# The first two groups of a gated linear attention kernel, worked in chunks of 128 steps in place of groups of 256

## The chip, the cores and the metric

One NeuronCore of one Trainium2 chip. The metric is the device time of one execution in microseconds, as the median of several runs. A profiled execution gives the trace; its span, from the first to the last instruction, is a little shorter than its device time.

## What is computed

Inputs: `q`, `k`, `v`, `alpha` of shape (4, 8, 768, 48) (batch, heads, steps, head dimension), all float32, and the weights `w_in` (384 x 1024), `A_log` (512) and `w_out` (512 x 384), which arrive as float64.

```python
for t in range(S):                        # attention, per batch and head
    state = alpha[t][:, None] * state + outer(k[t], v[t])
    y[t] = q[t] @ state
x = y laid out as (B, S, H*D)             # 384 wide
val, gate = split(x @ w_in)               # 512 each
for t in range(S):
    h = exp(A_log)[0] * h + val[t];  ys[t] = h      # the reference uses one decay
out = (gate * sigmoid(gate) * ys) @ w_out
```

## The kernel before

The function `fast` does the work; `general` is a second program for inputs that its checks turn away, and isn't touched. The 4 x 768 steps are 12 groups `m` of 256 steps, three groups to a batch, and a group is two chunks `c` of 128. Heads lie in pairs: four pairs `p` of two heads, 64 columns each of which 48 are used, so a chunk of one quantity is a tile of 128 rows (two heads) by 4 x 128 columns (pair, step).

The recurrence is taken apart through running products of alpha. For each group, `products(m)` (line 616) runs on DVE: a small multiply puts the start value into `first` (626), a memset sets alpha's first column of each pair to zero (627), a scan of 1024 columns makes `prod` (629), then `ratio` (636 or 638) and a reciprocal (640) are taken from its end, and a scan backwards of 1025 columns makes `inv` (641). Keys are multiplied by `inv` and queries by `prod` into `Z` (603). Then, chunk by chunk:

- `scores` (668): eight products on PE of keys and queries into two PSUM banks, `sc[0]` and `sc[1]`.
- `masks` (678): DVE multiplies bank 0 by the causal mask (687, called the near mask below); ACT copies bank 1 to SBUF (685) and POOL multiplies it there by the mask (686, the far mask). For chunk (0, 1) DVE does both (683).
- `keys` (659): PE turns the keys back, ACT copies them out (666).
- `values` (689): PE adds masked scores times v into `y`; its second half uses what POOL masked.
- `state` (713): PE adds to the running state `st`, ACT copies it out (722); `carried` (701) adds the part of `y` that comes from the earlier state.
- `join` (724): ACT copies `y` out, and eight small DMAs lay it out as `xT`.

`project`, `hidden`, `gate` and `output` (747 to 800) are the second half, on which PE works for most of the time. The weights' 64-bit words are turned into float32 by `low_word` on ACT, `high_word` on DVE and `word_sum` on POOL (508 to 535).

The first three groups, and no others, are loaded in their natural order and turned by PE: `natural_alpha` (572) and `natural_qk` (589). Alpha of a group is copied from PSUM into `aT` (584 on ACT, 586 on DVE); keys and queries are multiplied straight out of PSUM.

The whole is under a manual schedule: every engine runs its instructions in the order in which the program emits them, and waits where a tile isn't ready. For the start this order is written out in lines 814 to 902: the loads on SP (and two on ACT), the constants (476), then alpha of group 0, its products, keys and queries, group 1's first products, group 0's scores, masks, values and state, `join(0)`, the rest of group 1, `join(1)`. Between them stand six `warm` matmuls of 512 columns (827), whose results aren't used. [...]

Of the kernel before, what the change touches and what calls it, by code (L numbers as in the profile page):

```python
# [341 lines left out]
FIRST_PRODUCT = 1e18  # L342
# [4 lines left out]
def fast(  # L347
# [118 lines left out]
    alphas = aT[:, 0:4 * GC].rearrange("p (h n) -> p h n", h=4)  # L466
    prods = prod.rearrange("p (h n) -> p h n", h=4)
    invs = inv[:, 1:].rearrange("p (h n) -> p h n", h=4)
    ratio = const.tile([C, N, 4], FP32, name="ratio")
    above = const.tile([C, N], FP32, name="above")  # L470
    wmin = const.tile([C, NW], FP32, name="wmin")
# [2 lines left out]
    flag = const.tile([1, 1], I32, name="flag")  # L474

    def constants():
        for m, engine in ((0, nc.vector), (1, nc.gpsimd)):
            if m:
                make_identity(nc, ident)

                nc.gpsimd.memset(mask, 1.0)
                nc.gpsimd.affine_select(out=mask, in_=mask, compare_op=ALU.is_ge, fill=0.0, base=0,
                                        channel_multiplier=-1, pattern=[[1, C]])
                for t in vs:
                    nc.gpsimd.memset(t[:, :, :, D:64], 0.0)

            for name in "akq":
                engine.memset(natural(name, m)[:, :, :, D:64], 1.0)
        for t, x in ((minus, -1.0), (start_p, FIRST_PRODUCT), (aT[:, 4 * GC:], 0.0), (first, FLOOR),
                     (last, 0.0), (one, 1.0)):  # L490
            nc.vector.memset(t, x)
        for m in range(2):
            for name in "akq":
                nc.gpsimd.memset(raw_bufs[m][name].rearrange("p h n -> p (h n)")[:, G * H * 64:], 1.0)
# [74 lines left out]

    Zs = {}  # L570

    def natural_alpha(m, banks=None):

        tps = []
        for c in range(G):
            tp = (banks or ps_mm).tile([C, 4, C], FP32, tag=f"sc{c}" if banks else "mm", name="tn")
            for p in range(4):
                nc.tensor.transpose(tp[:, p, :], natural("a", m)[:, c, 2 * p:2 * p + 2, :], ident)
            tps.append(tp)

        def evict():
            for c in range(G):
                if m or not c:
                    nc.scalar.activation(alphas[:, :, ds(c * C, C)], tps[c], AF.Copy)
                else:
                    nc.vector.tensor_copy(out=alphas[:, :, ds(c * C, C)], in_=tps[c])
        return evict

    def natural_qk(m, name, banks=None):

        if m not in Zs:
            Zs[m] = p2.tile([C, 4, 2, GC], FP32, tag="Z", name="Z")
        tps = []
        for c in range(G):
            tp = (banks or ps_sc).tile([C, 4, C], FP32, tag="mm" if banks else f"sc{c}", name="tn")
            for p in range(4):
                nc.tensor.transpose(tp[:, p, :], natural(name, m)[:, c, 2 * p:2 * p + 2, :], ident)
            tps.append(tp)

        def times(c):  # L600
            i, by = {"k": (1, invs), "q": (0, prods)}[name]
            cols = ds(c * C, C)
            nc.vector.tensor_mul(Zs[m][:, :, i, cols], tps[c], by[:, :, cols])
        return times

    def check_alpha(m):

# [5 lines left out]
        junk = p1.tile([C, x, y, z], BF16, tag="junk", name="junk")  # L613
        nc.scalar.activation(junk, src, AF.Relu, bias=minus, accum_out=above[:, m:m + 1])

    def products(m):
        g = m % NG

        def turn(name, to):
            nc.vector.transpose(out=to.rearrange("p h (c j) -> p h j c", j=NT),  # L620
                                in_=raw_bufs[m % NR][name].rearrange("p h (j d) -> p h j d", d=D)[:, :, :, 0:32])

        if m >= NAT:
            check_alpha(m)
            turn("a", alphas)
        nc.vector.tensor_mul(first[:, :, 0], alphas[:, :, 0], prods[:, :, GC - 1] if g else start_p)
        nc.vector.memset(alphas[:, :, 0:1], 0.0)
        yield
        nc.vector.tensor_tensor_scan(  # L629
            out=prod, data0=aT[:, 0:4 * GC], data1=first.rearrange("p h n -> p (h n)"),  # L630
            initial=0.0, op0=ALU.mult, op1=ALU.max)
        yield

        end, inv_end = prods[:, :, GC - 1], last[:, 1:5, 0]
        if g:
            nc.vector.tensor_mul(ratio[:, m], end, inv_end)
        else:
            nc.vector.tensor_scalar(out=ratio[:, m], in0=end, scalar1=1.0 / FIRST_PRODUCT, scalar2=None,
                                    op0=ALU.mult)
        nc.vector.reciprocal(inv_end, end)  # L640
        nc.vector.tensor_tensor_scan(  # L641
            out=inv[:, ::-1], data0=aT[:, ::-1],
            data1=last.rearrange("p h n -> p (h n)")[:, 0:4 * GC + 1][:, ::-1],
            initial=0.0, op0=ALU.mult, op1=ALU.add)
        yield
        if m < NAT:
            return
        Z = Zs[m] = p2.tile([C, 4, 2, GC], FP32, tag="Z", name="Z")
        for name, i, by in (("k", 1, invs), ("q", 0, prods)):
            turn(name, Z[:, :, i])  # L650
            yield
            nc.vector.tensor_mul(Z[:, :, i], Z[:, :, i], by)
            yield
# [11 lines left out]
            nc.tensor.transpose(tp[:, p, :], Zs[m][:, p, 1, ds(c * C, C)], ident)  # L665
        nc.scalar.activation(ktms[c].rearrange("p a i d -> p a (i d)"), tp, AF.Copy)

    def scores(m, c):
        Z = Zs[m]
        cols = ds(c * C, C)  # L670
        sc = [ps_sc.tile([C, 4, C], FP32, tag=f"sc{i}", name=f"sc{i}") for i in range(2)]
        for p in range(4):
            for i in range(2):
                rows = ds(64 * i, D)
                nc.tensor.matmul(sc[i][:, p, :], Z[rows, p, 1, cols], Z[rows, p, 0, cols], start=True, stop=True)  # L675
        As[m, c] = p2.tile([C, 2, 4, C], FP32, tag="A", name="A"), sc

    def masks(m, c):
        A, sc = As[m, c]
        mb = mask[:, None, :].to_broadcast([C, 4, C])  # L680
        if (m, c) == (0, 1):
            for i in range(2):
                nc.vector.tensor_mul(A[:, i], sc[i], mb)
            return
        nc.scalar.activation(A[:, 1], sc[1], AF.Copy)  # L685
        nc.gpsimd.tensor_mul(A[:, 1], A[:, 1], mb)  # L686
        nc.vector.tensor_mul(A[:, 0], sc[0], mb)  # L687

    def values(m, c):
        v_sb = vs[m % NV]  # L690
# [118 lines left out]
    def pair(name, m, one, other):  # L809
        load_natural(name, m, 0, one)  # L810
        load_natural(name, m, 1, other)
# [1 line left out]

    pair("a", 0, SP, ACT)
    ACT.dma_start(out=a_log, in_=moe_A_log.rearrange("(a p) -> a p", p=C))
    pair("k", 0, SP, SP)
    pair("q", 0, SP, SP)
    pair("a", 1, SP, SP)
    load_v(0, SP)
    pair("k", 1, SP, SP)  # L820
    pair("q", 1, SP, SP)
    load_v(1, SP)
    for i in range(2):
        load_w_in(i, SP)

    constants()
    def warm(count):

        t = ps_mm.tile([C, 4, C], FP32, tag="mm", name="warm")
        for _ in range(count):  # L830
            nc.tensor.matmul(t, ident, ident[:, None, :].to_broadcast([C, 4, C]), start=True, stop=True)

    nc.scalar.activation(ok[:, 0:1], minus, AF.Exp)
    warm(2)


    evict = natural_alpha(0)
    al = ps_mm.tile([C, NI], FP32, tag="mm", name="al")
    nc.tensor.transpose(al, a_log, ident[0:NI, 0:NI])
    evict()  # L840
    nc.scalar.activation(a_dec, al, AF.Exp)
    check_alpha(0)
    k_times, q_times = natural_qk(0, "k"), natural_qk(0, "q")
    warm(2)
    evict = natural_alpha(1)
    warm(2)
    for _ in products(0):
        pass
    evict()
    check_alpha(1)  # L850
    steps = products(1)
    for c in range(G):
        k_times(c)
        q_times(c)
    next(steps)
    next(steps)
    for c in range(G):
        scores(0, c)
    nc.scalar.activation(ok[:, 0:1], minus, AF.Silu)
    for c in range(G):  # L860
        masks(0, c)
    for c in range(G):
        keys(0, c)
    values(0, 0)
    state(0, 0)
    values(0, 1)
    state(0, 1)
    carried(0, 1)
    join(0, (SP, nc.gpsimd))
    for i in range(2, NI):  # L870
        load_w_in(i, SP)
    for i in range(2):
        load_w_out(i, SP)
    k_times, q_times = natural_qk(1, "k"), natural_qk(1, "q", ps_mm)
    for _ in steps:
        pass

    for c in range(G):
        k_times(c)
        q_times(c)  # L880
    for c in range(G):
        keys(1, c)
        scores(1, c)
        masks(1, c)
    low_word(0)
    state(1, 0)
    values(1, 0)
# [24 lines left out]
        words(cc + 2)  # L912
        times()
    finish = output(0)
    natural_alpha(2, ps_sc)()
    check_alpha(2)
    loads(3)
    for _ in products(2):
# [5 lines left out]
    for n in range(1, N):  # L924
# [17 lines left out]

        if n == 1:
            block(n, 0)
            k_times, q_times = natural_qk(m, "k"), natural_qk(m, "q")
            for c in range(G):
                k_times(c)
                q_times(c)
            block(n, 1)

        if n + 3 < N:
# [78 lines left out]
```

## Time and profile before

| | us |
|---|---|
| median of 3 runs | 295.94 (295.72 to 296.15) |
| the profiled execution | 295.78 |
| its span | 294.1 |
| PE busy in the span | 284.2 (97%) |
| DVE busy in the span | 224.9 (76%) |
| POOL busy in the span | 115.9 (39%) |
| ACT busy in the span | 100.0 (34%) |
| DMA, mean over the span | 143 GB/s |

A line of the timeline has the start and the length in us, the engine, the line of the program, the operation, and the tile that is written and those that are read; "PEld" are PE's weight loads, and a bracket at the end says how long the engine stood idle before and what ended that. One float32 matmul of PE is two records. The other views are said where they are used.

### The profile page before, as it was taken

What the parts mean: (1) busy time and instruction counts of PE and PEld (TensorE: products, weight loads), DVE (VectorE), ACT (ScalarE), POOL (GpSimd) and SP (SyncE); (2) the same over time, 40 slices, a digit from 0 to 9 for tenths busy, and PEclk for the clock granted to TensorE, in tenths of its full rate; (3) what the DMA queues carried; (4) which work ended last, traced back from release to release, by engine and by line L of the source; (5) the groups of instructions that cost most, each with busy time, mean ns of one, the idle gap of its engine ahead of it and who ended that gap; (6) DMA issues with size and microseconds to landing.
All of it is one profiled execution on the core that took longest, in us unless ns stands there. A gap on an engine that the chain in (4) does not pass through costs nothing. (4 is left out here: it accounts for less than half of the span.)

```text
span 294.1 us, 6119 instructions
## 1 busy us (share of the span) xinstructions
PE 284.2 (97%) x2343; PEld 226.1 (77%) x2343; DVE 224.9 (76%) x262; ACT 100.0 (34%) x221; POOL 115.9 (39%) x114
## 2 busy tenths in 40 slices
PE   8899999999999999999999999999999999999991
PEld 4478887885896896886886886886886887886870
DVE  4997896999996799699699699699699695312211
ACT  3357534432432431431431431431531531431110
POOL 7026792375642613542513513543523452401110
PEclk9999999999999999999999999999999999999997
DMA  9999979999991991991891891891792401101101
GB/s 129 163 172 301 364 122 175 237 257 206 258 181 38 247 175 33 231 198 29 242 183 35 218 209 32 213 205 40 191 217 52 108 10 36 54 11 31 54 4 62
DMA packets 71230, 42.08 MB, mean 143 GB/s; under 512 B 47492, under 2 KB 70536, under 8 KB 71192
## 3 DMA queue, kind: packets, MB, share of 16 engines
q1 hardware_dynamic: 69760, 40.96, 68.4%
q0 software_dynamic: 384, 0.44, 0.7%
q8 instruction: 20, 0.33, 0.5%
q10 hardware_dynamic: 1048, 0.20, 0.4%
q14 instruction: 18, 0.15, 0.2%
HBM read 33.33 MB, written 4.72 MB: 129 GB/s over the span
## 5 line engine op out<-in xcount | busy, mean ns | idle before, releaser
L771 POOL TENSOR_TENSOR f<-sg,hh 128x256 f32<-128x256 f32 x48 | 63.3, 1319 | 93.0 <-ACT sg L770 45.6
L755 PE MATMUL pv<-xT,w_in 128*128 128x256 f32 x288 | 72.3, 387 | 0.0
L755 PE MATMUL pg<-xT,w_in 128*128 128x256 f32 x288 | 70.2, 380 | 0.0
L785 PE MATMUL o<-w_out,f 128*128 128x384 f32 x192 | 64.3, 487 | 0.5 <-DVE hh L763 0.5
L755 PEld LDWEIGHTS pg<-xT,w_in 128*128 128x128 f32 x288 | 54.6, 190 | 7.9 <-DVE hh L763 0.5
L755 PEld LDWEIGHTS pv<-xT,w_in 128*128 128x128 f32 x288 | 52.8, 190 | 10.0 <-issue 1.9
L686 POOL TENSOR_TENSOR A<-A,mask 128x512 f32<-128x512 f32 x23 | 29.3, 1293 | 68.3 <-ACT A L685 68.3
L785 PEld LDWEIGHTS o<-w_out,f 128*128 128x128 f32 x192 | 36.3, 190 | 23.5 <-DVE hh L763 1.1
L770 ACT ACTIVATE sg<-pg 128x256 f32<-128x256 f32 x48 | 18.4, 384 | 93.9 <-PE pg L755 89.3
L763 DVE TENSOR_TENSOR_SCAN hh<-a_dec,hh,pv 128x256 f32<-128x256 f32 x32 | 23.3, 727 | 23.9 <-PE pv L755 23.9
L629 DVE TENSOR_TENSOR_SCAN prod<-aT,first 128x1024 f32<-128x1024 f32 x12 | 32.3, 2695 | 0.1
L687 DVE TENSOR_TENSOR A<-sc,mask 128x512 f32<-128x512 f32 x23 | 15.7, 690 | 20.5 <-PE sc L675 20.3
L641 DVE TENSOR_TENSOR_SCAN inv<-aT,last 128x1025 f32<-128x1025 f32 x12 | 29.6, 2463 | 0.4
L793 ACT ACTIVATE o_sb<-o 128x384 f32<-128x384 f32 x22 | 10.8, 491 | 43.5 <-PE o L785 43.5
L675 PE MATMUL sc<-Z 48*128 48x128 f32 x384 | 24.9, 279 | 0.0
L675 PEld LDWEIGHTS sc<-Z 48*128 48x128 f32 x384 | 22.5, 188 | 2.9 <-issue 1.7
L698 PE MATMUL y<-A,v 128*64 128x128 f32 x384 | 23.7, 274 | 0.8 <-DVE A L687 0.6
L698 PEld LDWEIGHTS y<-A,v 128*64 128x64 f32 x384 | 20.7, 137 | 1.4 <-DVE A L687 0.9
L620 DVE STREAM_TRANSPOSE aT<-raw_a 128x1024 f32<-128x1024 f32 x9 | 18.4, 2040 | 0.7 <-DMA raw_a<-in_alpha_dram 0.7
L620 DVE STREAM_TRANSPOSE Z<-raw_q 128x1024 f32<-128x1024 f32 x9 | 18.2, 2022 | 0.0
L620 DVE STREAM_TRANSPOSE Z<-raw_k 128x1024 f32<-128x1024 f32 x9 | 18.2, 2017 | 0.0
L719 PEld LDWEIGHTS st<-v,ktm 128*64 128x64 f32 x320 | 11.4, 137 | 3.4 <-issue 3.0
(91 smaller groups left out, 266.5 us busy)
## 6 DMA issues: line engine op xcount, KB each, us to landing
raw_k<-in_k_dram SPq DMA_DIRECT2D x24, 192.0 KB, 5.2
raw_q<-in_q_dram SPq DMA_DIRECT2D x24, 192.0 KB, 6.3
v<-in_v_dram SPq DMA_DIRECT2D x24, 192.0 KB, 6.4
out_dram<-o_sb SPq DMA_DIRECT2D x24, 192.0 KB, 1.9
raw_a<-in_alpha_dram SPq DMA_DIRECT2D x23, 192.0 KB, 4.1
raw_a<-in_alpha_dram SPq DMA_DIRECT2D x18, 176.0 KB, 4.1
raw_k<-in_k_dram SPq DMA_DIRECT2D x18, 176.0 KB, 6.3
raw_q<-in_q_dram SPq DMA_DIRECT2D x18, 176.0 KB, 6.7
```

The lines of the kernel that those rows point to most:

```text
L620: nc.vector.transpose(out=to.rearrange("p h (c j) -> p h j c", j=NT), in_=raw_bufs[m % NR][name].rearrange("p h (j d) -> p h j d", d=D)[:, ...
L629: nc.vector.tensor_tensor_scan(out=prod, data0=aT[:, 0:4 * GC], data1=first.rearrange("p h n -> p (h n)"), initial=0.0, op0=ALU.mult, op1= ...
L641: nc.vector.tensor_tensor_scan(out=inv[:, ::-1], data0=aT[:, ::-1], data1=last.rearrange("p h n -> p (h n)")[:, 0:4 * GC + 1][:, ::-1], in ...
L675: nc.tensor.matmul(sc[i][:, p, :], Z[rows, p, 1, cols], Z[rows, p, 0, cols], start=True, stop=True)
L686: nc.gpsimd.tensor_mul(A[:, 1], A[:, 1], mb)
L687: nc.vector.tensor_mul(A[:, 0], sc[0], mb)
L698: nc.tensor.matmul(ys[m][i][ds(64 * s, 64), e, ds(c * C, C)], v_sb[:, c, 2 * p + i, :], A[:, i, p, :], start=(c == 0 and e == 0), stop=Fal ...
L755: nc.tensor.matmul(pj, w_in[cc][:, kk, vg, :], xT[:, kk, :], start=(kk == 0), stop=(kk == NK - 1))
L763: nc.vector.tensor_tensor_scan(out=hh, data0=a_dec[:, cc:cc + 1].to_broadcast([C, GC]), data1=pv, initial=prev_h[cc][:, GC - 1:GC] if n % ...
L770: nc.scalar.activation(sg, pg, AF.Silu)
L771: return lambda: nc.gpsimd.tensor_mul(fs[n][:, cc, :], sg, hhs.pop((n, cc)))
L785: nc.tensor.matmul(os[c], fs[n][:, cc, ds(c * C, C)], w_out[:, cc, :], start=(cc == 0), stop=(cc == NI - 1))
```

## The change

Three things are changed in the start; groups from 3 on are as before.

The products of groups 0 and 1 are made per chunk by `chunk_products`, with scans of 512 columns and their own slices of `first`, `last`, `prod` and `inv`. Group 0's scans read alpha in its PSUM bank, where the memset of the first columns also goes; group 1's alpha is copied to `aT` by ACT chunk by chunk. Group 2 goes back to the whole layout, with two extra small memsets.

The order at the start is rewritten: products, keys and queries, scores, masks of one chunk, then of the next. `masks` is split in `masks_far` and `masks_near`, and chunk (0, 1) is masked as the others are. `warm` goes; seven matmuls of 128 columns on the constant `first` come ahead of alpha, into the bank of `st`. The transposed decay goes through the same bank, and ACT's dummy Silu moves up behind it. The loads of k, q, v and of group 1's alpha go chunk by chunk.

```diff
-        for m, engine in ((0, nc.vector), (1, nc.gpsimd)):
...
+        nc.vector.memset(first, FLOOR)
+        make_identity(nc, ident)
+        for name in "akq":
+            nc.vector.memset(natural(name, 0)[:, :, :, D:64], 1.0)
...
+    def chunk_products(m, c, al):
+
+        by_place = lambda t: t.rearrange("p (h n) -> p h n", h=4)
+        al_0, flat = by_place(al)[:, :, 0], last_c[c].rearrange("p h n -> p (h n)")[:, 0:4 * C]
+        prod, inv = prod_c[c], inv_c[c]
+        nc.vector.tensor_mul(first_c[:, :, 0], al_0, ends[m, c - 1] if c else ends[m - 1, 1] if m else start_p)
+        nc.vector.memset(al_0, 0.0)
+        nc.vector.tensor_tensor_scan(out=prod, data0=al, data1=first_c.rearrange("p h n -> p (h n)"),
+                                     initial=0.0, op0=ALU.mult, op1=ALU.max)
+        yield
+        end, inv_end = by_place(prod)[:, :, C - 1], last_c[c][:, 1:5, 0]
+        ends[m, c] = end
+        if c and m:
+            nc.vector.tensor_mul(ratio[:, m], end, inv_end)
+        elif c:
+            nc.vector.tensor_scalar(out=ratio[:, m], in0=end, scalar1=1.0 / FIRST_PRODUCT, scalar2=None,
+                                    op0=ALU.mult)
+        nc.vector.reciprocal(inv_end, end)
+        nc.vector.tensor_copy(out=inv[:, 4 * C:], in_=last_c[c][:, 4, 0:1])
+        nc.vector.tensor_tensor_scan(out=inv[:, 0:4 * C][:, ::-1], data0=al[:, ::-1], data1=flat[:, ::-1],
+                                     initial=last_c[c][:, 4, 0:1], op0=ALU.mult, op1=ALU.add)
+        yield
...
+        if m == 2:
+            nc.vector.memset(first.rearrange("p h (c n) -> p (h c) n", c=2)[:, :, 0], FLOOR)
...
+        if m == 2:
+            nc.vector.memset(last.rearrange("p h (c n) -> p (h c) n", c=2)[:, :, 0], 0.0)
...
+    def masks_far(m, c):
         A, sc = As[m, c]
-        mb = mask[:, None, :].to_broadcast([C, 4, C])
-        if (m, c) == (0, 1):
-            for i in range(2):
-                nc.vector.tensor_mul(A[:, i], sc[i], mb)
-            return
         nc.scalar.activation(A[:, 1], sc[1], AF.Copy)
-        nc.gpsimd.tensor_mul(A[:, 1], A[:, 1], mb)
-        nc.vector.tensor_mul(A[:, 0], sc[0], mb)
+        nc.gpsimd.tensor_mul(A[:, 1], A[:, 1], mask_all())
+
+    def masks_near(m, c):
+        A, sc = As[m, c]
+        nc.vector.tensor_mul(A[:, 0], sc[0], mask_all())
...
-    pair("k", 0, SP, SP)
-    pair("q", 0, SP, SP)
-    pair("a", 1, SP, SP)
-    load_v(0, SP)
-    pair("k", 1, SP, SP)
-    pair("q", 1, SP, SP)
+    for c in range(G):
+        for name in "kq":
+            load_natural(name, 0, c, SP)
+    for c in range(G):
+        load_natural("a", 1, c, SP)
+        load_v(0, SP, [c])
+    for c in range(G):
+        for name in "kq":
+            load_natural(name, 1, c, SP)
...
+    t = st.rearrange("p h d -> p (h d)")[:, 0:C]
+    for _ in range(7):
+        nc.tensor.matmul(t, first_c[:, 0], first_c[:, 0], start=True, stop=True)
...
+    al = [alpha_bank(0, c).rearrange("p h n -> p (h n)") for c in range(G)]
+    tl = st[:, 0, 0:NI]
+    nc.tensor.transpose(tl, a_log, ident[0:NI, 0:NI])
+    nc.scalar.activation(a_dec, tl, AF.Exp)
+    nc.scalar.activation(ok[:, 0:1], minus, AF.Silu)
     check_alpha(0)
...
+    qk = turn_qk(0)
+    for fill, _ in qk:
+        fill()
+    for _ in chunk_products(0, 0, al[0]):
         pass
...
+    for _, times in qk[:2]:
+        times()
+    scores(0, 0)
+    masks_far(0, 0)
+    keys(0, 0)
+    steps = chunk_products(0, 1, al[1])
     next(steps)
+    masks_near(0, 0)
+    alpha_copy(0, alpha_bank(1, 0))
     next(steps)
...
+    for _, times in qk[2:]:
+        times()
+    banks = score_banks()
     values(0, 0)
+    scores(0, 1, banks)
+    masks_far(0, 1)
     state(0, 0)
+    keys(0, 1)
+    tp = alpha_bank(1, 1)
+    steps = chunk_products(1, 0, aT_c[0])
+    next(steps)
+    masks_near(0, 1)
+    alpha_copy(1, tp)
     values(0, 1)
     state(0, 1)
     carried(0, 1)
+    qk = turn_qk(1)
+    for fill, _ in qk[:2]:
+        fill()
     join(0, (SP, nc.gpsimd))
...
+    next(steps)
+    for _, times in qk[:2]:
+        times()
+    scores(1, 0)
+    masks_far(1, 0)
+    keys(1, 0)
+    for fill, _ in qk[2:]:
+        fill()
+    check_alpha(1)
+    steps = chunk_products(1, 1, aT_c[1])
+    next(steps)
+    masks_near(1, 0)
+    next(steps)
+    for _, times in qk[2:]:
+        times()
+    scores(1, 1)
+    masks(1, 1)
+    keys(1, 1)
     low_word(0)
     state(1, 0)
     values(1, 0)
```

## The prediction

> **What bounds the kernel now.** I read the page's part 2 first, then the busy time by stage, then the timeline of the first 32 us. Part 2 gives busy tenths in 40 slices of 7.35 us:
>
> ```profile
> PE   8899999999999999999999999999999999999991
> DVE  4997896999996799699699699699699695312211
> ```
>
> PE is full from the third or fourth slice to the end. The windows (us, then busy us and instruction count of PE, PEld, DVE, ACT, POOL) say the same of the stages:
>
> ```profile
> 8.00:12.00 4.00, 2.87 (x16) 1.71 (x15) 3.90 (x5) 0.25 (x2) 0.00 (x0) 1.00 1.53 163
> 16.00:20.00 4.00, 3.36 (x54) 2.93 (x52) 3.96 (x6) 2.31 (x5) 1.79 (x1) 1.00 1.50 166
> 90.00:270.00 180.00, 180.00 (x1517) 144.50 (x1516) 141.73 (x148) 59.13 (x137) 66.22 (x49) 1.00 0.58 124
> ```
>
> So the change, which works in the first 31 us, is worth what it does to one moment: the first projection (pv, line 755), after which PE is never short of work for long. It stands here in the timeline (start, length, engine, line):
>
> ```profile
> 7.03 0.69 DVE L586 COPY aT<-tn 128x512 f32<-128x512 f32 x1 [2.83 <-PE tn L578]
> 7.75 0.17 DVE L626 TENSOR_TENSOR first<-aT,start_p 128x4 f32<-128x4 f32 x1
> 8.09 2.29 DVE L629 TENSOR_TENSOR_SCAN prod<-aT,first 128x1024 f32<-128x1024 f32 x1
> ...
> 22.20 1.09 PE L597 MATMUL tn<-ident,raw_k 128*128 128x128 f32 x8
> 22.89 0.69 DVE L603 TENSOR_TENSOR Z<-tn,inv 128x512 f32<-128x512 f32 x1 [0.39 <-PE tn L597]
> ...
> 24.97 0.68 DVE L603 TENSOR_TENSOR Z<-tn,prod 128x512 f32<-128x512 f32 x1
> ...
> 27.30 0.67 PE L719 MATMUL st<-v,ktm 128*64 128x48 f32 x16
> ...
> 31.53 1.56 PE L755 MATMUL pv<-xT,w_in 128*128 128x256 f32 x6
> ```
>
> The chain: alpha is copied out, DVE works almost without a gap from 7.75 to 25.65 (end of the last Z), the scores follow (ready 27.30), then PE's own queue of state, values and carried terms, and pv at 31.53. DMA isn't last there: the inputs land every 1.2 us (192 KB at 163 GB/s), q's second chunk, the sixth, at 10.12, the last group 1 key or query before 20, all ahead of their use except that q. I call the end of the last Z "E"; E to pv is 5.9 us.
>
> **What the skill says.** (1) "GPSIMD Engine Reference", section 1, Specifications: POOL shares its SBUF interfaces with VectorE and contends with DVE instructions that have two SBUF inputs or run in a two-port mode. The trace agrees: with POOL's two masks running from 57.95 to 60.45, DVE's multiply of four columns took 0.99 us, not 0.17:
>
> ```profile
> 57.95 2.50 POOL L686 TENSOR_TENSOR A<-A,mask 128x512 f32<-128x512 f32 x2 [1.55 <-ACT A L685]
> 58.25 0.99 DVE L626 TENSOR_TENSOR first<-aT,start_p 128x4 f32<-128x4 f32 x1
> 63.52 0.51 DVE L638 TENSOR_SCALAR ratio<-prod 128x4 f32<-128x4 f32 x1
> ```
>
> The third line is the one-input ratio, 0.51 instead of about 0.15, under a POOL multiply that ends at 64.0. And POOL's first mask took 1.79, not 1.27, under a scan. (2) "VectorE: DVE Perf Modes", the TRN2 errata section: a fixed cost per instruction, so pieces cost more than the whole. The trace: a scan of 1024 takes 2.29, one of 256 takes 0.67. (3) "PSUM — Partial Sum Buffer", Engine vs sequencer instructions: matmuls start and complete in program order. The trace has them so. (4) "TensorE: Matmul & The Clock Gate", What's actually happening: an idle PE falls to half clock. The trace: 512-column records 0.853 us apart at 2.45, 3.30, 4.15, and 0.43 apart after 11.
>
> **The change part by part.**
>
> *Start of DVE's chain.* The copies of alpha out of PSUM go (ACT 0.60, DVE 0.69); the scan reads the bank. The new warm-up waits for the 1024-column memset (0.93+0.91, so 1.90), and its 7 matmuls of 128 columns are 14 records of 0.853/4=0.213: ends 4.89, where the old one ended at 5.00. Alpha has landed by 4.76 (first weight load). Four cold transposes to first use were 1.10 (5.00 to ACT's 6.10), so DVE starts at **6.0**, against 7.75: 1.75 earlier.
>
> *DVE's work for a chunk*, start to start: multiply 0.23 and memset 0.09 (15.50, 15.73, 15.82); scan of 512: 0.67 + 256 x (2.29-0.67)/768 = 1.21, with 0.03 to the next 1.24, from PSUM as from SBUF (the 256 one has a PSUM input); step one 1.56. Reciprocal 0.21 (20.00 to 20.21), the one-column copy 0.10 (between memset's 0.06 and the 0.17 of a small multiply), scan 1.24: step two 1.55, with a ratio 0.08 (group 0) or 0.19. Key and query products 0.60 each, near mask 0.60. A chunk is 4.9 to 5.1; four of them less the last mask 19.4. Before, 7.75 to 25.65 is 17.9, with one near mask fewer and the far mask of (0,1) in it. Moving that to ACT and POOL saves 0.60; halving the scans doubles everything small in a group. Net, DVE has more to do, not less.
>
> *Chunk (0,0):* 6.0+1.56+1.55+1.2=10.31. Scores (0,0) sit on PE behind the turn of q (0,1), which lands at 10.12: start 10.64, ready 11.93 (from 24.53 to 25.82 before: 1.29). *Chunk (0,1):* step one to 11.87, near mask 11.93 to 12.53. POOL's far mask starts 0.68 after the scores (25.82 to 26.50): 12.61 to 13.89. Ratio and copy start at 12.53 and 12.82, on top of it: a tie that I can't call. Below: no wait; above: all three behind POOL, 1.3. I take half, 0.6. The scan itself has a PSUM input and isn't stopped. Then 12.53+0.08+1.55+1.2+0.08+0.6: the last Z of group 0 ends at **X=16.05** (15.44 to 16.75).
>
> *The new stall.* PE's queue now has, behind scores (0,1): state, keys, alpha, values (0,1), state, carried, and only then the turn of group 1's first key, which DVE needs next. Values' second half waits for POOL: scores ready X+1.36, POOL X+2.04 to X+3.32, PE X+3.38; then half of values 0.38, state 0.54, carried 0.59, turn to DVE 0.69 (22.20 to 22.89): X+5.58. DVE alone would be there at X+3.63 (1.48+0.6+1.55). So it stands still 1.95; its scan, stopped by POOL till X+3.32, ends X+4.56 and is covered. Y, the end of Z for (1,0), is X+6.86.
>
> *Chunk (1,1).* Step one Y+1.48, mask Y+2.08; POOL's mask Y+2.04 to Y+3.32; ratio (two SBUF inputs) waits to Y+3.32, costing 1.24 (if it gets in first, the SBUF scan still waits: 0.75; below, none). Then 0.19+1.55+1.2+0.08: E=Y+6.34. Scores 0.07+1.09, then keys 0.52, now behind the scores, and 4.05 of state, values and carried (27.30 to 31.53 less 0.17 of POOL wait): pv = E+5.73 = X+18.93 = **34.98**, 3.45 later than 31.53.
>
> *Edits at nothing.* Silu's table load 1.28 moves to about 7.4 on ACT, followed by the alpha check 1.13, done by 10; ACT is first needed at 11.93 (without that cover up to 1.3). Alpha copies of group 1 on ACT end by 14 and X+4, needed X and Y. The later alpha check ends 4 us before ACT's last mask. SP issues the same 192 KB loads in another order; k (1,1) and q (1,1) keep the last two of group 1's places, the weights stay behind all of them. Join (0)'s four SP and four POOL DMAs come after y, X+4.9; POOL's 2.19 ends before its mask at Y+2.04; w_in 2 and 3 and w_out go out behind SP's and aren't waited for. POOL's sum of the first weight half is done 2.5 after the mask, ahead of pv. If a cover fails, the piece is under 1.3 each. Two strided memsets and the switch of layout for group 2 add 0.15 to DVE near 46, in a stretch to 70 in which PE waits 0.5 for DVE: taken in full.
>
> **Sum.** 3.45+0.15=3.6. Profiled execution 295.78 (span 294.1 and 1.68 around it): 299.4. The median of the runs is 0.16 above that execution; I leave it inside the range.
>
> **Rivals.**
> - *No lock:* POOL and DVE miss each other in both places. X=15.44, and 1.24 less: 3.6-0.6-1.24=1.75, 297.5. For: the ties are of 0.05 us. Against: the SBUF scan behind is caught anyway.
> - *No stall either:* PE reaches the key's turn in time; 1.95 less, 295.6, no change. Against: its order is written out.
> - *Faster:* the 1.75 of the early start gets through, because pieces cost only half of a whole scan (1.15) and the small instructions hide: 0.3 a chunk, 1.2 on top of the case before: 294.4. It decides when stall, locks and small work together cost under the 1.75. Against: 2.29 and 0.67 fix the price of a piece.
> - *Cold PE:* the four mid-way warm matmuls are gone; PE idles about 2.5 us before scores (1,1). If the clock falls, 3.4 us (the skill's window, (4)) of half-speed work add up to 1.7: 301.1.
>
> **How the numbers follow.** Forecast with locks (298.5 to 300.6) 0.50, no lock 0.22, no stall 0.09, faster 0.08, cold 0.11. Below 296.6 lie 0.15, above 301.2 about 0.05: range 296.6 to 301.2. A change of 0.2% (0.6 us) is about what a measurement can tell: faster 0.11 (its case and 0.03 of no stall), same 0.04, slower 0.85.
>
> **What would show it.** DVE's first small multiply at 6.0; a DVE wait of about 2 us for PE before group 1's first key product; a ratio of over 1 us beside POOL's mask; pv near 35. It is wrong if DVE shows no wait for the key's turn, if 512 scans take under 1.1, or if pv comes before 31.5.

## The result, and the profile after

The changed kernel takes 300.62 us (300.43 to 302.17), the one before 296.04 beside it: a ratio of 1.0167, 95% interval 1.0137 to 1.0196, so 4.6 us slower. The profiled execution is the slowest of those listed, 302.17 with a span of 300.4; why is said below.

The page's part 2 (busy tenths in 40 slices, here of 7.5 us; PEclk is PE's granted clock in tenths):

```profile
PE   7784999999999999999999999999999999999992
DVE  5969667899999599699699699699699697212211
PEclk9979599999999999999999999999999999999999
```

The clock of the kernel before, for comparison:

```profile
PEclk9999999999999999999999999999999999999997
```

PE is full from the fifth slice on (before, from the third), and only 4 tenths busy in the fourth. The third and fifth have a clock of 7 and 5 tenths, which no early slice had before. DVE is at 6 in the third, the fifth and the sixth. The timeline of DVE and PE in the start, in the order in which the work comes:

```profile
6.30 0.17 DVE L622 TENSOR_TENSOR first<-tn,start_p 128x4 f32<-128x4 f32 x1 [2.10 <-PE tn L581]
6.64 1.22 DVE L624 TENSOR_TENSOR_SCAN prod<-tn,first 128x512 f32<-128x512 f32 x1
...
12.81 0.16 DVE L632 TENSOR_SCALAR ratio<-prod 128x4 f32<-128x4 f32 x1
12.89 1.27 POOL L720 TENSOR_TENSOR A<-A,mask 128x512 f32<-128x512 f32 x1 [6.93 <-ACT A L719]
13.09 0.15 DVE L635 COPY inv<-last 128x1 f32<-128x1 f32 x1
...
15.07 0.68 DVE L602 TENSOR_TENSOR Z<-tn,prod 128x512 f32<-128x512 f32 x1
15.81 1.55 PE L707 MATMUL sc<-Z 48*128 48x128 f32 x16 [0.94 <-DVE Z L602]
18.32 1.12 PE L694 MATMUL tp<-ident,Z 128*128 128x128 f32 x4
22.82 0.69 DVE L602 TENSOR_TENSOR Z<-tn,inv 128x512 f32<-128x512 f32 x1 [2.36 <-PE tn L581]
...
26.07 0.16 DVE L630 TENSOR_TENSOR ratio<-prod,last 128x4 f32<-128x4 f32 x1
26.13 1.27 POOL L720 TENSOR_TENSOR A<-A,mask 128x512 f32<-128x512 f32 x1 [0.78 <-ACT A L719]
26.55 1.93 DVE L636 TENSOR_TENSOR_SCAN inv<-aT,last 128x512 f32<-128x512 f32 x1
29.19 0.68 DVE L602 TENSOR_TENSOR Z<-tn,prod 128x512 f32<-128x512 f32 x1
29.93 1.98 PE L707 MATMUL sc<-Z 48*128 48x128 f32 x16 [3.15 <-DVE Z L602]
...
33.77 3.46 PE L735 MATMUL y<-A,v 128*64 128x128 f32 x32
38.63 1.56 PE L792 MATMUL pv<-xT,w_in 128*128 128x256 f32 x6
```

Four things are to be read here. DVE starts at 6.30, 1.45 earlier than before. It then stands idle for 2.36 us until PE has turned group 1's first key (the bracket at 22.82). The backward scan at 26.55 takes 1.93, where the scan of the same length at 6.64 took 1.22: POOL's mask has started 0.42 before it. And scores (1,1) at 29.93 take 1.98, where 16 such records took 1.16 before, after a gap of 3.15 on PE. pv comes at 38.63 in place of 31.53.

The stages (us; busy us and instruction count of PE, PEld, DVE, ACT, POOL; then the granted clock, DMA share, GB/s) show what makes these scores slow:

```profile
12.00:16.00 4.00, 2.52 (x28) 1.87 (x28) 3.83 (x11) 1.64 (x3) 1.27 (x1) 1.00 1.53 163
16.00:20.00 4.00, 4.00 (x40) 3.57 (x38) 3.80 (x5) 1.46 (x3) 1.27 (x1) 0.57 1.51 166
28.00:32.00 4.00, 2.07 (x17) 1.85 (x18) 1.77 (x4) 0.00 (x0) 0.00 (x0) 0.76 0.96 306
32.00:36.00 4.00, 4.00 (x42) 3.67 (x44) 3.86 (x8) 3.05 (x5) 2.74 (x3) 0.50 1.03 402
36.00:40.00 4.00, 4.00 (x68) 3.63 (x65) 1.02 (x2) 1.61 (x4) 2.42 (x3) 0.89 0.10 38
```

PE ran at half clock in most of 16 to 20 and from 30 to almost 37. Of pv's 7.1 us, 6.3 reach the end of the span. The kernel before has one wait of PE for DVE after pv, which the changed one doesn't have; it makes up 0.5 of the difference:

```profile
68.94 3.49 PE L785 MATMUL o<-w_out,f 128*128 128x384 f32 x10 [0.51 <-DVE hh L763]
```

### The profile page after: what moved, and what is told of

It is laid out like the page before. It is cut to its first block, busy times and chain, and to the rows that moved or that the text cites. A ratio compares the mean times of both kernels' runs of the same rounds, so it can differ in the third digit from the quotient of the medians.

```text
span 300.4 us, 6133 instructions
## 1 busy us (share of the span) xinstructions
PE 285.4 (95%) x2345; PEld 230.6 (77%) x2345; DVE 227.6 (76%) x276; ACT 99.9 (33%) x221; POOL 112.2 (37%) x115
## 4 chain that ended last, share of the span: by engine, by line
PE 91%; DVE 4%; DMA 2%; SPq 1%; issue 0%; DVEq 0%
PE pv L792 22%; PE pg L792 21%; PE o L822 21%; PE sc L707 8%; PE y L735 7%; PE st L756 4%; PE y L746 3%; PE tp L694 3%; DMA raw_k<-in_k_dram 2%; DVE Z L602 2%; PE tn L581 2%; DVE inv L636 1%; DVE prod L624 1%; SPq L421 1%; DVE A L724 0%
## 5 line engine op out<-in xcount | busy, mean ns | idle before, releaser
L808 POOL TENSOR_TENSOR f<-sg,hh 128x256 f32<-128x256 f32 x48 | 59.0, 1229 | 96.6 <-DVE hh L800 51.1
L720 POOL TENSOR_TENSOR A<-A,mask 128x512 f32<-128x512 f32 x24 | 30.1, 1269 | 71.3 <-ACT A L719 71.3
L724 DVE TENSOR_TENSOR A<-sc,mask 128x512 f32<-128x512 f32 x24 | 16.4, 689 | 20.7 <-PE sc L707 20.7
L707 PE MATMUL sc<-Z 48*128 48x128 f32 x384 | 26.4, 288 | 5.2 <-DVE Z L602 5.0
L707 PEld LDWEIGHTS sc<-Z 48*128 48x128 f32 x384 | 23.5, 194 | 7.8 <-DVE Z L602 6.1
L656 DVE TENSOR_TENSOR_SCAN prod<-aT,first 128x1024 f32<-128x1024 f32 x10 | 28.4, 2835 | 0.0
L670 DVE TENSOR_TENSOR_SCAN inv<-aT,last 128x1025 f32<-128x1025 f32 x10 | 26.0, 2600 | 0.3
L735 PE MATMUL y<-A,v 128*64 128x128 f32 x384 | 25.2, 285 | 0.5 <-POOL A L720 0.5
L735 PEld LDWEIGHTS y<-A,v 128*64 128x64 f32 x384 | 22.3, 145 | 1.1 <-POOL A L720 0.8
L719 ACT ACTIVATE A<-sc 128x512 f32<-128x512 f32 x24 | 13.3, 598 | 13.3 <-PE sc L707 7.1
```

Source lines behind the costliest of these rows:

```text
L656: nc.vector.tensor_tensor_scan(out=prod, data0=aT[:, 0:4 * GC], data1=first.rearrange("p h n -> p (h n)"), initial=0.0, op0=ALU.mult, op1= ...
L670: nc.vector.tensor_tensor_scan(out=inv[:, ::-1], data0=aT[:, ::-1], data1=last.rearrange("p h n -> p (h n)")[:, 0:4 * GC + 1][:, ::-1], in ...
L720: nc.gpsimd.tensor_mul(A[:, 1], A[:, 1], mask_all())
L724: nc.vector.tensor_mul(A[:, 0], sc[0], mask_all())
L735: nc.tensor.matmul(ys[m][i][ds(64 * s, 64), e, ds(c * C, C)], v_sb[:, c, 2 * p + i, :], A[:, i, p, :], start=(c == 0 and e == 0), stop=Fal ...
L808: return lambda: nc.gpsimd.tensor_mul(fs[n][:, cc, :], sg, hhs.pop((n, cc)))
```

## The experiments

Each ratio is against the kernel before on the same chip, and is the middle of its interval; where only four executions were timed and scatter, it isn't the quotient of the medians. E (end of the last Z) and pv (start of the first projection) are of one profiled execution each, in us.

| kernel | us, median | ratio, 95% interval | E | pv | E to pv |
|---|---|---|---|---|---|
| before | 295.94 | | 25.65 | 31.53 | 5.9 |
| changed | 300.62 | 1.0167 (1.0137 to 1.0196) | 29.87 | 38.63 | 8.8 |
| changed, unused matmuls | 297.75 | 1.0058 (1.0043 to 1.0074) | 28.42 | 33.99 | 5.6 |
| changed, key turn ahead | 298.32 | 1.0110 (1.0041 to 1.0179) | 26.56 | 33.72 | 7.2 |
| changed, no POOL mask (1,0) | 300.22 | 1.0136 (1.0094 to 1.0178) | 27.76 | 36.52 | 8.8 |
| changed, unused matmuls and key turn | 296.12 | 0.9994 (0.9976 to 1.0012) | 26.40 | 32.13 | 5.7 |
| before, four unused matmuls out | 298.00 | 1.0099 (1.0059 to 1.0138) | 27.17 | 33.04 | 5.9 |
| rewritten tail | 295.56 | 0.9987 (0.9965 to 1.0009) | 26.12 | 31.69 | 5.6 |
| rewritten tail, state ahead | 295.62 | 1.0000 (0.9981 to 1.0020) | 26.13 | 31.32 | 5.2 |
| before, carried term ahead | 296.25 | 0.9999 (0.9978 to 1.0019) | 25.50 | 31.28 | 5.8 |

**Is it PE's clock?** Unused matmuls go back into the changed kernel's two gaps:

```diff
     alpha_copy(0, alpha_bank(1, 0))
+    warm_small(5)                      # ident times ident, 128 columns, into the bank of st
     next(steps)
...
     values(0, 0)
+    warm_small(2)
     scores(0, 1, banks)
...
     for fill, _ in qk[2:]:
         fill()
+    warm(3)                            # 512 columns
     check_alpha(1)
```

> The changed kernel with unused matmuls put back: seven of 128 columns between the alpha turn of (1,0) and scores (0,1), three of 512 before scores (1,1). Clock theory (half-speed PE is most of the loss): no record of scores (0,1) or (1,1) at half clock, scores (1,1) to pv down from 8.7 to about 5.7 us, the wait for group 1's first key from 2.4 to about 1.5, 296.5 to 298.0. Order theory (the queued key turn and the POOL lock are most of it): the clock recovers but the time stays within 1 us of the changed kernel's 300.6.

It came to 297.75, as the clock theory had it: it is 1.56 over the kernel before (296.19 on that chip) in place of 4.58, so 3.0 are back. Its granted clock is 1.00 in every stage of 4 us up to 40. Its timeline of PE and DVE:

```profile
21.37 0.69 DVE L602 TENSOR_TENSOR Z<-tn,inv 128x512 f32<-128x512 f32 x1 [1.29 <-PE tn L581]
...
25.10 1.93 DVE L636 TENSOR_TENSOR_SCAN inv<-aT,last 128x512 f32<-128x512 f32 x1
25.17 2.74 PE L877 MATMUL warm<-ident 128*128 128x512 f32 x6
28.47 1.16 PE L707 MATMUL sc<-Z 48*128 48x128 f32 x16 [0.56 <-DVE Z L602]
...
30.66 1.93 PE L735 MATMUL y<-A,v 128*64 128x128 f32 x32
```

Scores (1,1) are back at 1.16 and the 32 values records at 1.93 from 3.46. DVE's wait for the key is 1.29, not 2.36: in the changed kernel's profile PE did the work ahead of that turn at half clock too.

**Is it the order on PE?** The turn of group 1's first key and query goes ahead of values, state and carried terms of (0,1):

```diff
+    qk = [natural_qk(1, name, 0, i) for i, name in enumerate("kq")]
+    for fill, _ in qk:
+        fill()
     values(0, 1)
     state(0, 1)
     carried(0, 1)
-    qk = turn_qk(1)
-    for fill, _ in qk[:2]:
-        fill()
+    qk += [natural_qk(1, name, 1, i) for i, name in enumerate("kq")]
```

> The changed kernel with the turn of group 1's first key and query ahead of values, state and carried terms of (0,1) on PE. Order theory: DVE's wait before the first key product of (1,0) goes from 2.4 us to under 0.3, pv 2 to 2.5 us earlier, 298.1 to 298.6 if the half clock stays as it is. Clock theory: the half-clock stretch before scores (1,1) stays, so at most that 2.4 of the 4.6 comes back. If neither: DVE waits for something else (the scan behind POOL, the load of k) and the gain is under 1 us.

DVE's wait is gone, and so is the long scan that followed:

```profile
18.43 0.60 PE L581 MATMUL tn<-ident,raw_k 128*128 128x128 f32 x4
20.17 0.69 DVE L602 TENSOR_TENSOR Z<-tn,inv 128x512 f32<-128x512 f32 x1
23.90 1.27 DVE L636 TENSOR_TENSOR_SCAN inv<-aT,last 128x512 f32<-128x512 f32 x1
...
26.62 1.16 PE L707 MATMUL sc<-Z 48*128 48x128 f32 x16 [2.34 <-DVE Z L602]
27.71 1.08 PE L694 MATMUL tp<-ident,Z 128*128 128x128 f32 x4
...
29.61 2.71 PE L735 MATMUL y<-A,v 128*64 128x128 f32 x32
```

The first key product waits for nothing but DVE's own scan, and E is 26.56. The half clock stays: it sets in right after scores (1,1), which follow a gap of 2.34 on PE (values still 2.71, E to pv 7.2). The interval is wide, since its four timed executions lie between 297.15 and 301.52, with mean clocks of 0.992 to 0.976; by the medians 2.4 of the 4.6 us are back, by the interval anything from nothing to 3.4. So the half clock is no mere consequence of the stall: the gap on PE before scores (1,1) is DVE's work on a chunk, whenever that begins.

**Is it POOL holding the scan?** The far mask of (1,0) is left out:

```diff
-        nc.gpsimd.tensor_mul(A[:, 1], A[:, 1], mask_all())
+        if (m, c) != (1, 0):
+            nc.gpsimd.tensor_mul(A[:, 1], A[:, 1], mask_all())
```

> The changed kernel without POOL's multiply of the far bank of chunk (1,0): heads 1, 3, 5 and 7 of that chunk keep their scores of later steps, so that part of the masking is left out. Lock theory: the backward scan of (1,1) takes 1.25 us in place of 1.93, and the time falls by 0.6 to 0.8 us. If the long scan has another cause, it stays at 1.9 and the time stays within 0.2 us.

```profile
18.00 2.07 DVE L636 TENSOR_TENSOR_SCAN inv<-aT,last 128x512 f32<-128x512 f32 x1
21.36 0.69 DVE L602 TENSOR_TENSOR Z<-tn,inv 128x512 f32<-128x512 f32 x1 [1.29 <-PE tn L581]
...
25.09 1.28 DVE L636 TENSOR_TENSOR_SCAN inv<-aT,last 128x512 f32<-128x512 f32 x1
...
27.82 1.88 PE L707 MATMUL sc<-Z 48*128 48x128 f32 x16 [2.49 <-DVE Z L602]
```

The scan of (1,1), from 25.09, takes 1.28; the same scan in the run with unused matmuls, from 25.10, took 1.93 with the mask beside it. That of (1,0), beside which POOL's mask of (0,1) still runs, takes 2.07. So POOL is what lengthens it, by 0.65. In the time it shows as 0.55 (4.03 over the kernel before in place of 4.58), which the intervals don't separate from nothing. DVE's wait is 1.29 here as well, and the stage from 16 to 20 is at full clock in this execution: the first stretch at half clock comes in some executions and not in others, and with it 1.1 of the 2.36. The changed kernel's profiled execution has both stretches, a mean clock of 0.982 and a span of 300.4; its other executions have 0.985 to 0.987 and spans of 298.6 to 299.1, which fits the second stretch alone. That one, after the gap on PE, was there in all three profiles of a kernel that kept the gap empty.

**Both together.**

> Both of the first two: unused matmuls back and the key turn ahead. If stall and half clock add up, pv is within 1 us of the kernel before (31.5) and the time is 295.5 to 296.6, leaving the lock (0.7) and the work of the halved scans. If the half clock was only a consequence of the stall, it equals the run with the turn alone within 0.3 us.

296.12, and the ratio's interval holds 1. On top of the 3.0 for the clock, the turn is worth 1.6 more (297.75 to 296.12; pv goes from 33.99 to 32.13, about the stall of 1.29 and the long scan's 0.66). Whether it is worth as much without the clock repair, the scattered run with the turn alone can't say. The scan of (1,1) is short here too, though nothing was done to POOL's mask:

```profile
22.35 2.19 POOL L777 DMA_DIRECT2D xT<-y_sb  x4 [3.54 <-ACT y_sb L766]
23.73 1.27 DVE L636 TENSOR_TENSOR_SCAN inv<-aT,last 128x512 f32<-128x512 f32 x1
24.56 1.51 POOL L720 TENSOR_TENSOR A<-A,mask 128x512 f32<-128x512 f32 x1
```

The scan comes 1.4 earlier than with the unused matmuls alone (23.73, not 25.10), while `join`, now behind the turns on PE, comes 0.6 later (POOL's DMAs start at 22.35, not 21.71). POOL issues them until 24.54 and takes up the mask only after the scan has started. So the turn's 1.6 has both the stall and the lock in it.

**The same clock in the kernel before.** The four unused matmuls between the turn of group 0's keys and its scores are taken out:

```diff
     k_times, q_times = natural_qk(0, "k"), natural_qk(0, "q")
-    warm(2)
     evict = natural_alpha(1)
-    warm(2)
     for _ in products(0):
```

> The kernel before without the four unused matmuls of 512 columns that stand between the turn of group 0's keys and its scores. Clock theory, if these hold the clock up: a stretch at half clock between 12 and 20 us, scores and turns there twice as long, and 0.5 to 2 us more. If the matmuls that are left keep PE busy enough, because the kernel before has no gap of 3 us like the changed one's before scores (1,1): no half clock, and within 0.3 us or, as scores (0,0) needn't queue behind them, a little faster.

```profile
12.00:16.00 4.00, 2.62 (x18) 2.01 (x18) 3.79 (x8) 3.05 (x5) 0.00 (x0) 0.65 1.52 163
16.00:20.00 4.00, 4.00 (x31) 3.78 (x30) 3.95 (x6) 1.38 (x4) 1.27 (x1) 0.50 1.52 164
...
14.24 4.44 PE L675 MATMUL sc<-Z 48*128 48x128 f32 x32 [0.80 <-DVE Z L603]
```

Half clock from about 13 to 20 (the third line is the timeline's: group 0's scores, 4.44 in place of 2.06), pv at 33.04, 1.5 later, and 1.9 us more in the time by the medians (298.00 against 296.13; by the interval 1.7 to 4.1). So these four of the six 512-column matmuls that the change removes were worth that by themselves in the old order.

**Is there a version that beats both?** To the two repairs the tail was rewritten, with one unused matmul of 512 columns in it in place of three:

```diff
     steps = chunk_products(1, 1, aT_c[1])
     next(steps)
-    masks_near(1, 0)
     next(steps)
-    for _, times in qk[2:]:
-        times()
-    scores(1, 1)
-    masks(1, 1)
-    keys(1, 1)
     low_word(0)
+    qk[2][1]()
+    keys(1, 1)
     state(1, 0)
+    qk[3][1]()
+    scores(1, 1)
+    masks_near(1, 0)
+    masks_far(1, 1)
+    first_words(0)                     # DVE's work on half of the first weight unit
+    masks_near(1, 1)
+    first_words(1)
     values(1, 0)
+    carried(1, 0)
...
```

> Chunks with unused matmuls and the early key turn, and the tail rewritten: near mask of (1,0) after the last Z, keys (1,1), state and values of (1,0) and its carried term out of the way of the last scores, the first weight unit's DVE work in the wait for scores. E goes from 26.4 to about 25.8 and E to pv from 5.7 to about 4.9: pv near 30.7, 0.8 us before the kernel before, of which 0.3 to 0.8 us reach the end: 0.997 to 0.999 of the kernel before. If PE was not what ended last there, pv stays at 31.5 or later and there is no gain.

pv came at 31.69, not 30.7: E was 26.12, but scores (1,1) began only at 26.77, held by the state of (1,0) that I had put on PE in front of them, and everything behind followed. The next run moves `state(1, 0)` up, ahead of the last unused matmul:

> As the run before with the rewritten tail, but state (1,0) before keys (1,1), in PE's idle time, so that scores (1,1) start when the last Z is there (26.2) and not 0.65 us later (26.77). If that start sets POOL's mask and with it the end of PE's queue, pv comes at about 31.0 in place of 31.69 and the time is 0.996 to 0.998 of the kernel before. If POOL or the weights' sums end last by themselves, pv stays near 31.7.

Scores began at 26.40, pv at 31.32, and the span is 293.2 against 294.1 before; but the timed ratio is 1.0000. As a control, the kernel before with `carried(1, 0)` ahead of `values(1, 1)`:

> The kernel before with the carried term of chunk (1,0) ahead of values (1,1), so that it runs while PE waits for POOL's mask: nothing of chunks. If the tail of PE's queue ends last, pv comes 0.3 to 0.5 us earlier and the time falls by as much; then a gain of the rewritten chunks isn't all due to chunks. If POOL's sum of the first weights ends last, no change within 0.1 us.

pv is 0.25 earlier, of which 0.15 is an earlier start of DVE's chain in that execution (7.60, not 7.75), and the time is the same. None of the three is shown to beat the kernel before. With the state ahead pv is 0.21 earlier, without it 0.16 later than before; that is about the scatter of DVE's start (6.10 to 6.30 in profiles with the same start) and less than these intervals hold, about 0.6 us to each side. The expected gains didn't come.

## Why the prediction was right, and where it was off

The direction and the range (slower; 296.6 to 301.2) held, and the two causes in the sum, the queued turn and POOL's lock, were there. The single time of 299.4 was 1.2 too low, and that it is so near is in part luck, as the sum at the end shows. Point by point:

- *DVE's start:* 6.0 said, 6.30 measured. The warm-up began at 2.06 in place of 1.90, since DVE's first memset came 0.16 later, and alpha's turn with it; the other 0.14 isn't explained.
- *DVE's price of a chunk:* a scan of 512 was put at 1.21 and took 1.22 from PSUM and 1.23 from SBUF, forwards; 1.27 backwards. That DVE has more to do and not less is shown by the run with both repairs: it starts at 6.10 and ends at 26.40, 20.3 us, of which 0.8 is a held scan (2.09); 19.4 of work had been said, and the kernel before took 17.9. The gain at the start is spent there, and nothing of it is left at pv.
- *The tie in chunk (0,1):* half of 1.3 was put in. The ratio came 0.08 ahead of POOL's mask, reciprocal and copy ran beside it unhindered (13.09, 0.15), and it cost nothing. Whether the ratio would have been held behind the mask was thus not tested. X was 15.75, in the stated span.
- *The stall before the first key:* said at X+5.58, with a wait of 1.95. Where PE kept its clock the product came at X+5.60 (21.36 with X at 15.76), with a wait of 1.29, since the scan ahead of it was itself held by POOL as predicted, until 20.1. In the changed kernel's own profile it came at X+7.07, the rest being half clock. Moving the turn removed it: the cause is shown.
- *POOL's lock in chunk (1,1):* 1.24 was put in for a ratio behind the mask; the ratio got in 0.06 ahead, the case for which the text had 0.75. The scan lost 0.65.
- *E to pv:* 5.73 was said. It is 5.73 in the run with both repairs and 5.6 with the clock repaired, but 8.76 in the changed kernel.

The term that was mis-sized most is PE's clock. The text had it as a rival with a chance of 0.11 and up to 1.7 us, and nothing for it in the sum. It wasn't a rival to the queue and the lock but came on top of them, and it is the largest part: 3.0 of the 4.6 us. The gap that brings it was seen ("PE idles about 2.5 us before scores (1,1)"), and it was 3.15. The Trainium skill, "TensorE: Matmul & The Clock Gate", in What's actually happening, has the clock fall after an idle window of about 3.4 us and come back after a busy one. The runs agree on the length but not on the idleness: gaps of 3.15, 2.49 and 2.34 us (changed, no mask of (1,0), key turn ahead) all ended in half clock, and the last section shows falls after stretches of 3.4 us in which PE worked for up to 1.93.

The terms that were in the sum came to less than was said. The run with unused matmuls alone shows them, because it keeps the turn's place and the lock and has no half clock. Its pv is at 33.99, 1.0 before the 34.98 of the forecast: X came 0.3 earlier (the tie's 0.6, less the later start), chunk (1,1) took 0.6 less (the lock), and the way from E to pv 0.2 less. Then the forecast let all of pv's delay reach the end and put 0.15 on top, but of 2.46 us at pv 1.56 reached the median, in part because PE's wait near 69 is gone. So these terms made 1.6 us, not 3.6; the clock's 3.0 came on top, and 299.4 is near 300.62 because an omission of 3.0 met an excess of 2.0 (the other 0.2 is the kernel before, 296.04 here in place of 295.78).

## What to carry to other kernels

Before you split a long scan to start the next engine sooner, ask whether the engine that scans has slack. Here DVE had none: each half brought its own small instructions, 17.9 us from its start to E became 19.5 (a held scan apart), and even with the repairs no version was shown to be faster. After such a split follow the other queues too: the turn that the next chunk needed stood behind a wait of the chunk before (1.29 us), and a mask on POOL held a scan with two SBUF inputs (0.65 us). And count how busy a new order leaves PE: ten unused matmuls gave back 3.0 of the 4.6 us.

## What was not expected of the hardware

- PE's clock fell with gaps of 2.3 to 3.2 us on PE, and in the kernel before without its four unused matmuls with no gap over 0.8. The length of a gap is thus not what decides. In short windows of the traces the changes of the clock lie 3.4 us apart, or two or three times that: at 16.42, 19.84, 30.08 and 36.91 in the changed kernel, 27.79 and 31.20 with the key turn ahead, 28.07 and 34.90 without the mask of (1,0), 13.22 and 20.04 in the kernel before without the four matmuls. Laying steps of 3.41 us through these times, from 4 to 290 us, PE's busy time (turns counted as work) in each step at full clock sorts all of them:

| kernel | lowest busy steps, from (us): busy of 3.41 us | clock in the next step |
|---|---|---|
| changed | 13.01: 1.93; 26.66: 0.27 | half |
| changed | 23.25: 2.50; 6.18: 2.56 | full |
| key turn ahead | 24.37: 1.17 | half |
| key turn ahead | 7.31: 2.36; 14.13: 2.40 | full |
| no mask of (1,0) | 24.66: 0.92 | half |
| no mask of (1,0) | 7.59: 2.31; 14.42: 2.46 | full |
| before, four unused matmuls out | 9.81: 1.73 | half |
| before, four unused matmuls out | 6.39: 2.36 | full |

  After 1.93 or less the clock fell, after 2.31 or more it held. The steps begin at another time in each execution, which also explains why the stretch from 16 to 20 comes in one profile and not in another: with the same gaps there, the changed kernel's step had 1.93, and the steps of the run without the mask 2.88 and 2.46. This is read from five falls in four profiles; no run was made to test it, and between 1.93 and 2.31 it says nothing. The clock came back after one such step in two cases and after two in three; what decides that stays open.
- A reciprocal and a copy with one SBUF input ran at their usual 0.17 and 0.15 beside POOL's mask, though the one-input ratio of the kernel before had taken 0.51 beside a POOL multiply (why they differ is open), while two-input scans were held for 0.66 to 0.91 (1.93 to 2.18 in place of 1.27).
- POOL's issuing of four DMAs, 2.2 us, delayed its mask past the start of the scan, and so took the lock away. With the turn ahead, alone or with the unused matmuls, the scan takes 1.27, and the mask beside it 1.51 in place of 1.27.
